# A mixed attention and gated-MLP kernel: x loaded in whole rows, key weights by feature rows, gates of two segments at a time, and a new order

## The chip, the cores and the metric

The kernel runs on one core of a Trainium2 chip. A core has five engines with an instruction stream each: TensorE (PE, matrix products into PSUM), VectorE (DVE), ScalarE (ACT), GpSimd (POOL) and SyncE (SP, which here only issues transfers). Transfers run on 16 DMA engines; SP and ACT each feed a queue of them. Engines wait for each other by semaphores. The metric is the device time of one execution in microseconds.

## The reference

x is 2048 tokens of 512 features, in four segments of 512 tokens. One branch is attention with 32 heads of 16 features, causal inside a segment, plus a linear-attention memory that carries over from segment to segment; the other is a gated MLP. A sigmoid of x times gate_w mixes them for each token.

```python
g = sigmoid((x * gate_w).sum(-1, keepdims=True))
# a: for each segment s, with phi(t) = where(t > 0, t + 1, exp(t))
a_dot = softmax(q_s @ k_s.T * 0.25 + causal) @ v_s
a_mem = (phi(q_s) @ M) / (phi(q_s) @ z + 1e-6)
o_s   = sigmoid(beta) * a_mem + (1 - sigmoid(beta)) * a_dot
M, z  = M + phi(k_s).T @ v_s, z + phi(k_s).sum(tokens)
a = o @ wo
b = (gelu(x @ w_gate) * (x @ w_up)) @ w_down        # 512 -> 1792 -> 512
return g * a + (1 - g) * b
```

## The kernel before

Everything is a list of named tasks, and the engines' streams are cut from one order of all tasks that stands in the file as text (`ORDER`, from line 852). A word such as `Q0_1a:2` places the task Q0_1a and gives its PSUM bank; `Kev0_0:a` says that ACT does this eviction, `:d` that DVE does. `Sched.schedule` (line 120) reads it, and `Emitter` (line 143) derives from the tiles that each instruction reads and writes which semaphore it waits for. Nothing is decided at run time: an engine takes its instructions in the order of the text.

Names of tasks carry the segment first. K, Q, V are projections (`project`, line 467): a product of 4 matmuls, 512 columns wide, in two tasks a and b, into one of four PSUM banks (`psD`), and an eviction (Kev, Qev, Vev). kpada and kpadb spread the keys under masks into kD. `st` (line 595) are score products, four at a time on 32 rows of the array, into the one large PSUM buffer `psX`; `exp` (line 601) turns 2048 columns of it on ACT into `pt`, `msk` (line 607) masks on POOL, and `pv` (line 638) multiplies with the values. The next `st` may only write psX when the `exp` before has read it. G and U are the two MLP products, `gd` and `gelu` the gelu on ACT, `h` (line 687) their product on DVE, `out` (line 700) the product with w_down, `wo` (line 716) the product with wo; `wev` scales the MLP part by 1 - g, `oev` (line 720) adds g times the attention part, and `dma` (line 723) stores 128 tokens. `mz`, `nz` and `nd` are the memory's products; `phk`, `phq` the feature map phi in three steps a, b, c; `ktr` its transpose by DMA; `vsh` (line 501) a copy of the values shifted by 64 partitions.

At the start x of segment 0 is loaded into a free `pt` buffer in four pieces of 256 tokens by 256 features, two on SP and two on ACT, and wk in four pieces of 256 feature rows by 256 columns, interleaved with them; wq follows in four pieces on SP. `turn_x0` (line 766) transposes x on TensorE (`xtr0`), two pieces at a time, and DVE and ACT evict it to xT (`xev0`). The key product of segment 0 (line 475) runs in eight tasks: 128 key features by 256 tokens each. Until the weights are there, TensorE runs matmuls on constants (`wake0`, `wake1`, line 366). x of the segments 1 to 3 comes by four transposing transfers each (`ld_xt`, line 328).

What stands behind each other on SP: four pieces of x and wk, four of wq, wv (waits for the last piece of x), beta, gate_w, the halves of wg (the first waits for wq, the second for wv), the four transposed pieces of x of segment 1, four vsh, then wu and the rest.

`gates` (line 412) computes g for one segment: 16 matmuls with one column of gate_w as the stationary operand into four partitions of a bank, a 32 by 32 block transpose and a minimum on DVE (`gz`), exp on ACT (`gr`), and three small steps on DVE (`go`) to g and 1 - g. gate_w itself is loaded as four rows, transposed by TensorE (`gwtr`, line 742) and copied by DVE (`gwev`).

At the end, output tile 15 alone is made and stored in two halves, one from SP and one from ACT.

Of the kernel before, what the change touches and what calls it, by code (L numbers as in the profile page):

```python
# [10 lines left out]
F32 = mybir.dt.float32  # L11
# [224 lines left out]
def _build(es, nc, A_x, A_wq, A_wk, A_wv, A_wo, A_beta, B_w_gate, B_w_up, B_w_down, gate_w, out):  # L236
# [39 lines left out]
    gt = sb("gt", [P, P], F32)  # L276
# [31 lines left out]
    def bk(s):  # L308
        return ("bank", s)
# [12 lines left out]
    gw4, ball = omem[0:4, 0, 0:P], omem[:, 1, 0:H]  # L322
    stage = (R_PT - 1,)

# [3 lines left out]
    def ld_xt(s, behind="wo30"):  # L328
        for kb in range(4):
            load(f"x{s}_{kb}", SP, lambda e, kb=kb: e.dma_start_transpose(  # L330
                xT[s % R_XT][:, kb, :], A_x[0, s * 512:(s + 1) * 512, kb * 128:(kb + 1) * 128]),
                [("xT", s % R_XT, kb, h) for h in range(2)], issue=1.31, size=0.28, wait=[("ld", behind)])
# [6 lines left out]
    for nm, w, a in (("wk", wk, A_wk), ("wq", wq, A_wq)):  # L339
        for h in range(2):  # L340
            c = slice(256 * h, 256 * h + 256)
            for k, eng in enumerate((SP, ACT if nm == "wk" else SP)):
                ld_w(f"{nm}{h}{k}", eng, w[:, halves[k], c], wsrc(a)[:, halves[k], c], [(nm, h, k)], 0.125)
    ld_w("gw", SP, gw4, gate_w.rearrange("(kb p) -> kb p", p=P), [("gw4",)], 0.01, ["x0_10"])
    ld_w("wv", SP, wv[:], wsrc(A_wv), [("wv",)], 0.5, ["x0_11"])
    ld_w("beta", SP, ball, A_beta.partition_broadcast(P), [("ball",)], 0.02, ["wk00"])
    ld_xt(1, "wv")
    ld_w("wg0", SP, wg[:, halves[0], :], wgr[:, halves[0], :], [("wg", 0)], 0.9, ["wq11"])
# [63 lines left out]
    def gates(s):  # L412
        sl = Slot()
        c = slice(4 * s, 4 * s + 4)

        mm = []
        for kb in range(4):
            for i in range(4):
                mm.append(I(lambda e, i=i, kb=kb: e.matmul(  # L419
                    BK[sl.i][32 * i:32 * i + 1, 0:128], gatew[:, kb:kb + 1],  # L420
                    xT[s % R_XT][:, kb, :].rearrange("p (q j r) -> p j q r", j=4, r=32)[:, i],
                    start=(kb == 0), stop=(kb == 3), tile_position=(0, 32 * i)),
                    [*x_of(s % R_XT, kb), ("gatew",)], [bk(sl)]))
        one(f"gate{s}", PE, 0.26, mm)
        one(f"gz{s}", DVE, 0.36, [
            I(lambda e: e.transpose(gt[:, :], BK[sl.i][:, 0:128]), [bk(sl)], [("gt",)]),
            I(lambda e: e.tensor_scalar(gz[:, c], gt[:, 0:128:32], ZMAX, None, ALU.min), [("gt",)], [("gz", s)])])
        one(f"gr{s}", ACT, 0.2, [I(lambda e: e.activation(gr[:, c], gz[:, c], ACTF.Exp), [("gz", s)], [("gr", s)])])
        one(f"go{s}", DVE, 1.2, [
            I(lambda e: e.tensor_scalar(gr1[:, c], gr[:, c], 1.0, None, ALU.add), [("gr", s)], [("gr1", s)]),  # L430
            I(lambda e: e.reciprocal(omgt[:, c], gr1[:, c]), [("gr1", s)], [("omgt", s)]),
            I(lambda e: e.tensor_tensor(gtok[:, c], gr[:, c], omgt[:, c], ALU.mult), [("gr", s), ("omgt", s)],
              [("gtok", s)]),
        ])

    def x_of(i, kb):
        return [("xT", i, kb, h) for h in range(2)]
# [29 lines left out]
    def project(s):  # L467
        b, b3 = s % 2, s % R_XT
        for t in range(4):
            if s == 0:  # L470

                sl = Slot()
                for h in range(2):
                    c = slice(256 * h, 256 * h + 256)
                    one(f"K0_{t}{'ab'[h]}", PE, 2 * T_MM, [I(lambda e, i=i, t=t, c=c, sl=sl: e.matmul(  # L475
                        BK[sl.i][:, c], wk[:, i, t * 128:(t + 1) * 128], xT[0][:, i, c], start=(i == 0), stop=(i == 3)),
                        [("xT", 0, i, h), ("wk", t // 2, i // 2)], [bk(sl)]) for i in range(4)])
            else:
                sl = dense(f"K{s}_{t}", lambda i, t=t: wk[:, i, t * 128:(t + 1) * 128], lambda i: xT[b3][:, i, :],
                           lambda i, t=t: [*x_of(b3, i), ("wk", t // 2, i // 2)], 4)  # L480
# [3 lines left out]
            for nm, ap, mk in (("kpada", kD[b][:, t, :, 0:64], maskA), ("kpadb", kD[b][:, t, :, 64:128], maskB)):  # L484
# [4 lines left out]
                       lambda i, t=t: [*x_of(b3, i), ("wq", t // 2, i // 2)], 4)  # L489
# [14 lines left out]
        gates(s)  # L504
# [50 lines left out]
    def memory_write(s):  # L555
# [3 lines left out]
        for t in range(4):  # L559
# [4 lines left out]
        sl = Slot()  # L564
        one(f"mz{s}", PE, 0.45, [I(lambda e, c=c, kt=kt, g=g, sl=sl: e.matmul(  # L565
# [10 lines left out]
                [("mzacc",), ("gphm",)], [("mzq",)])])  # L576
        one(f"zq{s}", POOL, 0.25, [I(lambda e: e.tensor_tensor(
# [112 lines left out]
    def outputs(s):  # L690
        for qt in range(4):
# [4 lines left out]
            for pi, (a, z) in enumerate(((0, 3), (3, 6), (6, 8), (8, 11), (11, 14))):  # L696
                mm = []
                for fb in range(a, z):
# [8 lines left out]
                    [bk(sl), ("omgt", s)], [("wds", wi)])]),  # L707
                (DVE, 0.66, [I(lambda e, sl=sl, gt=gt, wi=wi: e.tensor_scalar(
                    wds[wi][:, :], BK[sl.i][:, :], omgt[:, gt:gt + 1], None, ALU.mult),
                    [bk(sl), ("omgt", s)], [("wds", wi)])])], L_DVE)  # L710
            last = gt == 4 * NSEG - 1
            parts = (slice(0, 256), slice(256, 512)) if last else (slice(0, 512),)
            ko = [[("ost", oi, 0)], [("ost", oi, 1)]] if last else [[("ost", oi, 0), ("ost", oi, 1)]]
            for ci, c in enumerate(parts):
# [7 lines left out]
                        op0=ALU.mult, op1=ALU.add), [bk(so), ("gtok", s), ("wds", wi)], ko[ci])])  # L722
                one(f"dma{gt}_{ci}", (SP, ACT)[ci], 0.5, [I(lambda e, gt=gt, oi=oi, c=c: e.dma_start(
                    out[0, gt * 128:(gt + 1) * 128, c], ost[oi][:, c]), ko[ci], [("out", gt, ci)],
                    dma_sem=sem(f"s_out{gt}_{ci}"))], lat=2.0)
                outs.append(f"s_out{gt}_{ci}")
# [3 lines left out]
    def head_gates():  # L730
# [10 lines left out]
        sg = Slot()  # L741
        one("gwtr", PE, T_TR, [I(lambda e: e.transpose(BKbf[sg.i][:, 0:4], gw4, ident[0:4, 0:4]),
                                 [("gw4",), ("omem", 0), ("ident",)], [bk(sg)])])
        one("gwev", DVE, 0.1, [I(lambda e: e.tensor_copy(gatew[:, :], BKbf[sg.i][:, 0:4]), [bk(sg)], [("gatew",)])])
# [21 lines left out]
    def turn_x0():  # L766
        xs = pt[stage[0]]
        xbf = XALL.bitcast(BF)
        for h in range(2):
            for k in range(2):  # L770
                sl = Slot() if h == 0 else None
                key, held = (bk(sl), []) if h == 0 else (("Xq", k), [("X", s0)])
                dst_of = (lambda sl=sl: BKbf[sl.i][:, 0:512]) if h == 0 else (
                    lambda k=k: xbf[:, 1024 * k + 1024:1024 * k + 1536])
                one(f"xtr0_{2 * h + k}", PE, 4 * T_TR, [I(lambda e, q=q, kb=kb, dst_of=dst_of: e.transpose(
                    dst_of()[:, 256 * (kb % 2) + 128 * (q % 2):256 * (kb % 2) + 128 * (q % 2) + 128],
                    xs[:, q, kb * 128:(kb + 1) * 128], ident[:, :]), [("xs", 0, h, k), ("pt", stage[0]), ("ident",)],
                    [key]) for kb in (2 * k, 2 * k + 1) for q in (2 * h, 2 * h + 1)])
                dst = xT[0][:, halves[k], 256 * h:256 * h + 256]
                src = lambda dst_of=dst_of: dst_of().rearrange("p (k c) -> p k c", k=2)  # L780
                wr = [("xT", 0, kb, h) for kb in (2 * k, 2 * k + 1)]
                task(f"xev0_{2 * h + k}", [
                    (ACT, 0.477, [I(lambda e, dst=dst, src=src: e.activation(dst, src(), ACTF.Copy), [key, *held], wr)]),
                    (DVE, 0.335, [I(lambda e, dst=dst, src=src: e.tensor_copy(dst, src()), [key, *held], wr)])], L_DVE)
# [3 lines left out]
    for s in range(NSEG):  # L788
        if s == NSEG - 1:
            ld_xt(s)  # L790
# [62 lines left out]
ld_x0_00 ld_x0_01 ld_wk00 ld_wk01 ld_x0_10 ld_x0_11 ld_wk10 ld_wk11 ident causal1 causal0 consts masks wake0:0 ld_wq00  # L853
ld_wq01 ld_wq10 ld_wq11 ld_wv ld_beta ld_gw ld_wg0 ld_wg1 ld_x1_2 ld_x1_1 ld_x1_0 ld_x1_3 causal vones0 xtr0_0:0
xtr0_1:3 xev0_0:d xev0_1:a wake1 K0_1a:1 K0_0a:2 xtr0_2 xtr0_3 xev0_2:d xev0_3:a K0_2a:3 K0_3a:0 K0_0b K0_1b K0_2b
K0_3b Kev0_0:a Kev0_2:d Kev0_1:a kpadb0_1 phka0_0 Q0_1a:2 Q0_0a:1 Q0_0b Kev0_3:a phkb0_0 kpada0_0 kpada0_1 phka0_2
# [104 lines left out]
```

## Time and profile before

| | |
|---|---|
| runs, us | 266.31, 265.62, 266.41; median 266.31 |
| profiled execution | 266.57 us, span of its instructions 264.8 us, TensorE clock 1.00 |
| TensorE busy | 255.4 us of the span, 2792 matmuls |
| VectorE, ScalarE, GpSimd busy | 204.7, 207.2, 95.6 us |
| dearest group off TensorE | exp, 72 x 1.876 us = 135.1 us |
| DMA | 14.92 MB, HBM reads 8.14 MB, most of it in the first 60 us |

The span runs from the first to the last instruction; the time of a run is a little longer. TensorE's matmuls are pipelined: a 512-column matmul shows as 380 ns, but the next one starts 216 ns later, so a busy share says little by itself, and the start times and waits have to be read. A line such as `x8` merges eight instructions. The number in brackets behind it is how long the engine was idle before, and who released it.

### The profile page before, as it was taken

To read this page: it belongs to the slowest core of one execution; us is meant where nothing else is said; L and a number is where in the kernel's file an instruction comes from. 1 tells how busy PE (TensorE), PEld (TensorE's weight loads), DVE (VectorE), ACT (ScalarE), POOL (GpSimd) and SP (SyncE) were. 2 spreads that over 40 slices of the span, in tenths; PEclk is the share of its full clock that TensorE was granted. 3 is DMA by queue.
4 is the path that set the end of the run, shared out by engine and by line. 5 is a ranking of instruction groups with operands and counts; after the bars stand their busy time and mean duration, and the time that the engine had idled before them with its cause. 6 is when DMAs were issued, how large, how long until landed. Compare 5 with 4: busy or idle time off the path is not lost.

```text
span 264.8 us, 6603 instructions
## 1 busy us (share of the span) xinstructions
PE 255.4 (96%) x2792; PEld 112.4 (42%) x2830; DVE 204.7 (77%) x389; ACT 207.2 (78%) x170; POOL 95.6 (36%) x159
## 2 busy tenths in 40 slices
PE   7999999999999999999999999999999999999995
PEld 4634434444444443444434344444344443444442
DVE  1557576678967669999797998897987797958975
ACT  2689879988899988979988978658889967376601
POOL 6005514046422734052254438422635035062600
DMA  6895238950045020000103000013011000010002
GB/s 196 261 219 136 80 69 146 248 154 2 0 68 108 4 62 20 2 2 1 22 0 89 15 2 2 20 42 41 2 34 33 2 2 0 2 59 2 20 2 79
DMA packets 25251, 14.92 MB, mean 56 GB/s; under 512 B 14086, under 2 KB 24198, under 8 KB 25222
## 3 DMA queue, kind: packets, MB, share of 16 engines
q1 hardware_dynamic: 23990, 13.91, 23.3%
q10 hardware_dynamic: 1232, 0.59, 0.8%
q8 instruction: 22, 0.36, 0.6%
q14 instruction: 7, 0.06, 0.1%
HBM read 8.14 MB, written 2.10 MB: 39 GB/s over the span
## 4 chain that ended last, share of the span: by engine, by line
PE 88%; DVE 5%; issue 2%; DMA 2%; ACT 1%; SPq 1%; DVEq 0%; ACTq 0%
PE psD L450 49%; PE psD L700 18%; PE psX L595 8%; PE psD L638 5%; PE psD L716 5%; DMA wk<-in_A_wk_dram 2%; DVE gb L687 1%; PE psD L475 1%; DVE kT L443 1%; PE psD L565 1%; ACT pt L601 1%; SPq L326 1%; DVE oT L657 1%; DVE tT L518 0%; PE psD L419 0%
## 5 line engine op out<-in xcount | busy, mean ns | idle before, releaser
L601 ACT ACTIVATE pt<-psX 128x2048 bf16<-128x2048 f32 x72 | 135.1, 1876 | 32.3 <-PE psX L595 31.7
L607 POOL TENSOR_TENSOR pt<-pt,ctri 128x256 bf16<-128x256 bf16 x128 | 90.5, 714 | 152.8 <-ACT pt L601 148.4
L450 PE MATMUL psD<-xT,wu 128*128 128x512 bf16 x212 | 55.5, 380 | 1.6 <-issue 1.3
L450 PE MATMUL psD<-xT,wg 128*128 128x512 bf16 x217 | 54.8, 380 | 1.0 <-issue 0.5
L700 PE MATMUL psD<-wd,gb 128*128 128x512 bf16 x214 | 52.5, 379 | 1.4 <-issue 1.0
L687 DVE TENSOR_TENSOR gb<-psD,gb 128x512 bf16<-128x512 f32 x56 | 37.4, 682 | 12.0 <-PE psD L450 11.6
L518 DVE STREAM_TRANSPOSE tT<-psD 128x512 f32<-128x512 f32 x35 | 23.4, 694 | 11.4 <-PE psD L638 11.2
L700 PEld LDWEIGHTS psD<-wd,gb 128*128 128x128 bf16 x224 | 20.7, 98 | 25.8 <-issue 2.8
L450 PEld LDWEIGHTS psD<-xT,wg 128*128 128x128 bf16 x224 | 20.3, 98 | 26.1 <-issue 2.8
L450 PEld LDWEIGHTS psD<-xT,wu 128*128 128x128 bf16 x224 | 20.1, 98 | 25.5 <-issue 3.7
L595 PE MATMUL psX<-qT,kD 32*128 32x192 bf16 (+7 forms) x512 | 28.6, 287 | 0.2
L595 PEld LDWEIGHTS psX<-qT,kD 32*128 32x128 bf16 x512 | 8.2, 92 | 25.9 <-ACT pt L601 19.5
L649 DVE SCALAR_TENSOR_TENSOR ob<-tT,gq,rc 128x256 bf16<-128x256 f32 x32 | 18.2, 567 | 1.1
L638 PE MATMUL psD<-pt,vnat 64*17 64x128 bf16 (+7 forms) x512 | 18.7, 283 | 0.0
L443 DVE CAST gb<-psD 128x512 bf16<-128x512 f32 x23 | 15.7, 683 | 3.7 <-PE psD L450 3.6
L638 PE MATMUL psD<-pt,vsh 64*17 64x128 bf16 (+7 forms) x512 | 18.3, 283 | 0.0
L450 PE MATMUL psD<-wv,xT 128*128 128x512 bf16 x61 | 17.3, 381 | 0.3 <-issue 0.3
L450 PE MATMUL psD<-xT,wq 128*128 128x512 bf16 x62 | 16.7, 380 | 0.1
L716 PE MATMUL psD<-wo,oT 128*128 128x512 bf16 (+1 forms) x66 | 15.7, 366 | 0.3 <-issue 0.2
L638 PEld LDWEIGHTS psD<-pt,vnat 64*17 64x17 bf16 x512 | 11.6, 86 | 8.7 <-issue 3.8
L678 ACT ACTIVATE gb<-psD 128x512 bf16<-128x512 f32 x28 | 14.7, 602 | 0.3 <-PE psD L450 0.3
L720 DVE SCALAR_TENSOR_TENSOR ost<-psD,gtok,wds 128x512 bf16<-128x512 f32 (+1 forms) x17 | 11.9, 712 | 2.5 <-PE psD L716 2.2
(99 smaller groups left out, 251.2 us busy)
## 6 DMA issues: line engine op xcount, KB each, us to landing
out_dram<-ost SPq DMA_DIRECT2D x15, 128.0 KB, 1.7
wg<-in_B_w_gate_dram SPq DMA_DIRECT2D x2, 896.0 KB, 6.5
wu<-in_B_w_up_dram SPq DMA_DIRECT2D x2, 896.0 KB, 5.5
wd<-in_B_w_down_dram SPq DMA_DIRECT2D x2, 896.0 KB, 7.5
vsh<-vnat SPq DMA_DIRECT2D x16, 68.0 KB, 2.1
wq<-in_A_wq_dram SPq DMA_DIRECT2D x4, 128.0 KB, 4.7
wv<-in_A_wv_dram SPq DMA_DIRECT2D x1, 512.0 KB, 3.8
pt<-in_A_x_dram SPq DMA_DIRECT2D x2, 128.0 KB, 3.5
```

What stands on the lines that cost most here:

```text
L443: (DVE, 0.60, [I(lambda e: e.tensor_copy(dst, src()), [bk(sl), *reads], writes)]),
L450: one(f"{name}{'abcd'[h // 2]}", PE, 2 * T_MM, [I(lambda e, i=i: e.matmul(BK[sl.i][:, :], lhs(i), rhs(i), start=(i == 0), stop=(i == n - 1 ...
L518: one(f"tp{name}", DVE, 0.605, [I(lambda e, ts=ts, bank=bank: e.transpose(tT[ts.i][:, :], bank()), [key], [("tT", ts)])])
L595: ins.append(I(lambda e, c=c, kb=kb, ncol=ncol, c0=c0, g=g: e.matmul(XALL[:, g * 512 + c0:g * 512 + c0 + ncol], kD[b][quad(g), c, kb, :], ...
L601: one(f"exp{s}_{name}", ACT, 2048 * 0.000833 + 0.05, [I(lambda e: e.activation(pt[slot][:, :, :], xin, ACTF.Exp, scale=ATT_SCALE), [("X", ...
L607: ins.append(I(lambda e, mv=mv: e.tensor_tensor(mv, mv, cm, ALU.mult), [("pt", slot), ("causal",)], [("pt", slot)]))
L638: ins.append(I(lambda e, kb=kb, slot=slot, c0=c0, n=n, g=g, c=c, r0=r0, sl=banks[j], va=va: e.matmul(BK[sl.i][32 * c:32 * c + 17, 64 * kb: ...
L649: I(lambda e, ts=ts, t=t, j=j, dst=dst: e.scalar_tensor_tensor(out=dst, in0=t_rows(ts, 16), scalar=gq[:, 2 * t + j:2 * t + j + 1], in1=rc_ ...
L678: one(f"gd{s}_{ft}", ACT, 0.485, [I(lambda e, gi=gi, f=f, sl=sl: e.activation(gb[gi][:, f, :], BK[sl.i][:, :], ACTF.Gelu_apprx_tanh), [bk( ...
L687: one(f"h{s}_{ft}", DVE, 0.605, [I(lambda e, sl=sl, gi=gi, f=f: e.tensor_tensor(gb[gi][:, f, :], BK[sl.i][:, :], gb[gi][:, f, :], ALU.mult ...
L700: mm.append(I(lambda e, fb=fb, gi=gi, f=f, q=q, sl=sl: e.matmul(BK[sl.i][:, :], gb[gi][:, f, q], wd[:, fb, :], start=(fb == 0), stop=(fb = ...
L716: one(f"wo{s}_{qt}_{ci}", PE, 4 * T_MM / len(parts), [I(lambda e, kb=kb, q=q, so=so, c=c: e.matmul(BK[so.i][:, c], oT[:, kb, q], wo[:, kb, ...
```

## The change

x of segment 0 is loaded in four pieces of 128 tokens with whole rows (1 KB each), in turn from SP and ACT; wk in four pieces of 128 feature rows with all 512 columns (1 KB rows), after x, and wq in two. On each of the two queues both pieces of x stand ahead of both pieces of wk. wv waits for the third piece of x instead of the last, and the first half of wg for the first half of wq.

```diff
+    for q in range(4):
+        ld_w(f"x0_{q}", (SP, ACT)[q % 2], pt[stage[0]][:, q, :], A_x[0, 128 * q:128 * q + 128, :], [("xs", q)], 0.125)
+    for i in range(4):
+        ld_w(f"wk{i}", (SP, ACT)[i % 2], wk[:, i, :], wsrc(A_wk)[:, i, :], [("wk", i)], 0.125)
     for h in range(2):
-        for k, eng in enumerate((SP, ACT)):
-            c = slice(256 * k, 256 * k + 256)
-            ld_w(f"x0_{h}{k}", eng, pt[stage[0]][:, halves[h], c],
-                 A_x[0, 256 * h:256 * h + 256, c].rearrange("(q p) d -> p q d", p=P), [("xs", 0, h, k)], 0.125)
...
-    ld_w("gw", SP, gw4, gate_w.rearrange("(kb p) -> kb p", p=P), [("gw4",)], 0.01, ["x0_10"])
-    ld_w("wv", SP, wv[:], wsrc(A_wv), [("wv",)], 0.5, ["x0_11"])
+        ld_w(f"wq{h}", SP, wq[:, halves[h], :], wsrc(A_wq)[:, halves[h], :], [("wq", h)], 0.25)
+    load("gw", SP, lambda e: e.dma_start(gatew[:, :], gate_w.rearrange("(kb p) -> p kb", p=P),
+                                         allow_slow_non_contiguous=True), [("gatew",)], wait=[("ld", "x0_2")])
+    ld_w("wv", SP, wv[:], wsrc(A_wv), [("wv",)], 0.5, ["x0_2"])
```

x is transposed piece by piece, four transposes and one eviction each; in the new order DVE does all four evictions, the first piece goes through a bank and the others through psX. The key product of the first 256 tokens runs feature row block by feature row block over all four banks at once; the other 256 tokens follow key block by key block. The constant matmuls are nine ahead of the first transpose and none later.

```diff
+        if s == 0:
+            k0 = [Slot() for _ in range(4)]
+            for i in range(4):
+                one(f"K0_k{i}", PE, 2 * T_MM, [I(lambda e, i=i, t=t: e.matmul(
+                    BK[k0[t].i][:, 0:256], wk[:, i, t * 128:(t + 1) * 128], xT[0][:, i, 0:256], start=(i == 0),
+                    stop=(i == 3)), [("xT", 0, i, 0), ("xT", 0, i, 1), ("wk", i)], [bk(k0[t])]) for t in range(4)])
...
-    for i, cols in enumerate(([512] * 5 + [128] * 2, [128] * 6)):
+    for i, cols in enumerate(([512] * 5 + [128] * 3, [128] * 1)):
```

The gates of the segments 0 and 1, and of 2 and 3, are computed together: 32 matmuls into the upper half of the bank in which the memory product `mz` of segment 0 or 1 is then made, and one visit of each DVE and ACT step. gate_w comes by one transfer of 512 single elements, straight into the layout that the matmuls need; its transpose and copy are gone.

```diff
-    def gates(s):
-        sl = Slot()
-        c = slice(4 * s, 4 * s + 4)
...
+    def gate_products(h, sl):
+        one(f"gate{h}", PE, 0.5, [I(lambda e, i=i, kb=kb, s=s: e.matmul(
+            BK[sl.i][32 * i:32 * i + 1, 256 + 128 * (s % 2):384 + 128 * (s % 2)], gatew[:, kb:kb + 1],
+            xT[s % R_XT][:, kb, :].rearrange("p (q j r) -> p j q r", j=4, r=32)[:, i],
+            start=(kb == 0), stop=(kb == 3), tile_position=(0, 32 * i)),
+            [*x_of(s % R_XT, kb), ("ld", "gw")], [bk(sl)])
+            for s in (2 * h, 2 * h + 1) for kb in range(4) for i in range(4)])
...
+        if s < 2:
+            gate_products(s, sl)
```

(Here the `s` of the call is 0 or 1 and stands for the pair.) At the end, output tile 14 is made in two halves as well, and stored whole; tile 15 is made and stored in halves as before.

```diff
+            split = gt >= 4 * NSEG - 2
             last = gt == 4 * NSEG - 1
-            parts = (slice(0, 256), slice(256, 512)) if last else (slice(0, 512),)
+            parts = (slice(0, 256), slice(256, 512)) if split else (slice(0, 512),)
```

`ORDER` is another text throughout: banks, engines of the evictions and the place of nearly every task differ. Its start, and the part around the first read of x of segment 1 (`Q1_3a`):

```diff
+ld_x0_0 ld_x0_1 wake0:0 ident wake1 xtr0_0:2 ld_x0_2 ld_x0_3 xtr0_1 xtr0_2 xev0_0:d xev0_1:d ld_wk0 xtr0_3 ld_wk2
+xev0_3:d ld_wk1 K0_k0:2013 xev0_2:d K0_k1 ld_wk3 K0_k2 K0_k3 ld_wq0 K0_3b ld_wq1 K0_2b ld_wv Kev0_3:d Kev0_2:a phka0_2
+K0_0b masks Kev0_0:d K0_1b Kev0_1:a ld_beta phkb0_2 Q0_3a:3 kpadb0_1 Q0_0a:1 ld_wg0 Q0_0b consts causal1 Qev0_0:a
...
+Vev0_0:d V0_3b V0_2a:0 st0_0B:0 phkc0_2 V0_2b Vev0_2:d ld_x1_1 Vev0_3:a G0_2a:1 G0_1a:3 exp0_0B G0_1b Gev0_1:a G0_3a:2
+ld_x1_0 st0_0C:0 Q1_3a:0 G0_0a:3 G0_2b Gev0_2:d G0_3b ld_x1_3 exp0_0C Q1_3b msk0_0B phka0_0 vsh0_01 vsh0_21 Gev0_3:d
```

On SP the new gate_w transfer stands behind three of the four vsh of segment 0, and ahead of the fourth and of the second half of wu; the rest of SP's row has the same order up to the first transfer of x of segment 3. The count of ScalarE's table loads is the same in both orders.

More of the change, by code (lines that the diff above doesn't have):

```diff
@@ L321, in _build, with x_of @@
     halves = (slice(0, 2), slice(2, 4))
-    gw4, ball = omem[0:4, 0, 0:P], omem[:, 1, 0:H]
+    ball = omem[:, 1, 0:H]
     stage = (R_PT - 1,)
+    def x_of(i, kb):
+        return [("xT", i, kb, q) for q in range(4)]
     def ld_w(name, eng, dst, src, writes, size, wait=()):
@@ L409, in _build @@
     one("consts", POOL, 4.2, cn)
-    def gates(s):
-        sl = Slot()
-        c = slice(4 * s, 4 * s + 4)
[L416 to L433, printed above, removed]
-        ])
@@ L721, in outputs @@
                         out=ost[oi][:, c], in0=BK[so.i][:, c], scalar=gtok[:, gt:gt + 1], in1=wds[wi][:, c],
[L722 to L726, printed above, removed]
+                        op0=ALU.mult, op1=ALU.add), [bk(so), ("gtok", s // 2), ("wds", wi)], ko[ci])])
+                if last or ci == len(parts) - 1:
+                    kd, d = (ko[ci], c) if last else ([k for kk in ko for k in kk], slice(0, 512))
+                    one(f"dma{gt}_{ci}", (SP, ACT)[last and ci], 0.5, [I(lambda e, gt=gt, oi=oi, d=d: e.dma_start(
+                        out[0, gt * 128:(gt + 1) * 128, d], ost[oi][:, d]), kd, [("out", gt, ci)],
+                        dma_sem=sem(f"s_out{gt}_{ci}"))], lat=2.0)
+                    outs.append(f"s_out{gt}_{ci}")
     outs = []
@@ L768, in turn_x0 @@
         xbf = XALL.bitcast(BF)
[L769 to L784, printed above, removed]
+        for q in range(4):
+            sl = Slot() if q == 0 else None
+            key, held = (bk(sl), []) if q == 0 else (("Xq", q), [("X", s0)])
+            dst_of = (lambda sl=sl: BKbf[sl.i][:, 0:512]) if q == 0 else (lambda q=q: xbf[:, 1024 * q:1024 * q + 512])
+            one(f"xtr0_{q}", PE, 4 * T_TR, [I(lambda e, q=q, kb=kb, dst_of=dst_of: e.transpose(
+                dst_of()[:, 128 * kb:128 * kb + 128], xs[:, q, kb * 128:(kb + 1) * 128], ident[:, :]),
+                [("xs", q), ("pt", stage[0]), ("ident",)], [key]) for kb in range(4)])
+            dst = xT[0][:, :, 128 * q:128 * q + 128]
+            src = lambda dst_of=dst_of: dst_of().rearrange("p (k c) -> p k c", k=4)
+            wr = [("xT", 0, kb, q) for kb in range(4)]
+            task(f"xev0_{q}", [
+                (ACT, 0.477, [I(lambda e, dst=dst, src=src: e.activation(dst, src(), ACTF.Copy), [key, *held], wr)]),
+                (DVE, 0.335, [I(lambda e, dst=dst, src=src: e.tensor_copy(dst, src()), [key, *held], wr)])], L_DVE)
     turn_x0()
@@ L788, in _build @@
     for s in range(NSEG):
[L789 to L790 removed]
+        if s == 1:
+            ld_xt(3)
         project(s)
```

206 lines of the change are left out of this document (100 added, 106 removed).

## The prediction

> **What bounds the kernel now.** I read the page's busy shares first, then TensorE's own waits from 9.9 us to the end, then its timeline at the start, the transfers of the first 20 us and VectorE's timeline at the end.
>
> ```profile
> span 264.8 us, 6603 instructions
> ...
> PE 255.4 (96%) x2792; PEld 112.4 (42%) x2830; DVE 204.7 (77%) x389; ACT 207.2 (78%) x170; POOL 95.6 (36%) x159
> ```
>
> ```profile
> PE psD L450 <- issue: 2.1, 13, 0.2
> PE psD L700 <- issue: 1.0, 6, 0.2
> PE psD L450 <- DVE gb L687: 0.5, 3, 0.2
> PE psD L450 <- DVE oT L657: 0.2, 1, 0.2
> ```
>
> The second fence is the list of TensorE's waits between 9.9 and 262 us: name, total, times, longest. No idle time is over 0.2 us, about the 0.216 us pitch of one 512-column matmul, so most of these are single records that the trace lost. From the first query projection on, TensorE runs without a stall. Time can come from three places only: the start, TensorE's own work, and what follows its last matmul; and every new wait in between is paid in full.
>
> ```profile
> 3.61 0.83 PE L775 MATMUL psD<-ident,pt 128*128 128x128 bf16 x8 [0.25 <-DMA pt<-in_A_x_dram]
> ...
> 4.74 1.22 PE L475 MATMUL psD<-xT,wk 128*128 128x256 bf16 x8
> 6.21 0.79 PE L775 MATMUL psX<-ident,pt 128*128 128x128 bf16 x8 [0.24 <-DMA pt<-in_A_x_dram]
> 7.11 3.01 PE L475 MATMUL psD<-xT,wk 128*128 128x256 bf16 x24
> 10.17 3.40 PE L450 MATMUL psD<-xT,wq 128*128 128x512 bf16 x15
> ```
>
> TensorE's timeline (start, length): eight key matmuls run at 4.74, then it waits for the second half of x (6.21) and for wk (7.11). From 7.54 to 10.12 the chain of waits has 22 of them, so the pitch is 0.11; the last 24 end at 9.95. Of 16 query matmuls 15 are recorded; 16 x 0.216 back from the value matmul at 13.41 also gives **9.95** as the start of Q0.
>
> **The start (gain 1.0; ends 0.2 and 1.3).**
>
> ```profile
> wk<-in_A_wk_dram ACTq DMA_DIRECT2D x1, 128.0 KB, 5.1
> ...
> q1 hardware_dynamic: 548, 0.26, 111.0%
> ...
> q1 hardware_dynamic: 139, 0.14, 80.7%
> ```
>
> The first line is the last quarter of wk, issued at 2.39: landed at 2.39 + 5.1 = 7.5. The other two are the SP queue in windows 6.0 to 6.9 (512-byte packets) and 8.5 to 9.0 (1 KB): packets, MB, share of 16 engines. A packet took 0.9 x 16 x 1.11 / 548 = 29 ns, against 0.5 x 16 x 0.807 / 139 = 46 ns; a kilobyte so costs 58 ns before and 46 now, a factor of 0.79. First bytes flowed at about 2.2, so x and wk took 5.3 us; times 0.79 is 4.2, landing at 6.4. Part of it is the landing, which does not shrink: I take **6.7**. Ends: 7.5 (no gain) and 5.2 (1,024 packets x 46 ns / 16 = 2.9 us, engines never idle).
> The Trainium skill, "DMA: Bandwidth & Descriptors", section Specifications, puts the smallest transfer for line rate at 512 B, which would make the new rows no quicker; the two rows above disagree with it, and by the rule the sum would be 0.8 smaller.
>
> The rest of the new start: the first piece of x (issued at 0.81, 2.8 us to landing) is there at 3.6, as before. VectorE evicted the first transposes 0.65 us after they began (4.26); now it does all four evictions at 0.42 each, from 4.3: 4.7, 5.1, 5.5, 5.9. The first key group needs two pieces and the first 128 feature rows: 5.15. Four groups of 4 x 0.11 would end at 6.9; the fourth waits for 6.7, so it runs 6.75 to 7.2. The 16 matmuls of the second token half take 1.74: Q0 at **8.95** instead of 9.95. With all weights early it is 5.15 + 32 x 0.109 = 8.65, with wk at 7.5 it is 9.7. The longer first wake (nine matmuls, not seven) ends at about 3.4, before x; the filler it replaces ran in idle time. ScalarE loses its two x evictions, and its table load (1.28 us at 2.91) stays under the DMAs. The score group at the end of V0 needs eight key paddings and the evictions of K and Q: VectorE has 8 x 0.28 + 3 x 0.65 + 0.4 + 0.35 = 4.9 us for the 5.4 us between its first key eviction and TensorE's arrival, so this is tight but covered; without cover it costs 0.3.
>
> **TensorE's work after that (0.7 less; ends 0.3 and 0.9).** Each gate of 16 matmuls costs 0.33 in the chain of waits, 1.3 for four. Two of 32 remain, directly ahead of the memory product, which uses tiles of the same shape: 0.33 + 0.18 less a drain of about 0.1 each, 0.9 in all: 0.4 less. The small transpose of gate_w goes: its neighbours start 0.42 apart instead of 0.216, 0.2 less. Counted over both orders, changes of tile shape fall from 177 to 173; three belong to the gates, one more at 0.1 (a score group starts 0.31 after a dense matmul, 19.78 to 20.09).
> VectorE loses two gate visits (0.3 + 0.19 + 0.27 + 0.18 + 0.16 each) and a copy; it is 77% busy, so nothing comes of that. The gate weights now arrive as 512 elements of 2 bytes, issued on SP behind three of the four transfers of shifted values, about 20 us; behind them wait the fourth and wu. The fourth is first read at about 28, and its like took 2.1 us to land, so even 5 us more is hidden; gate0 itself runs at about 53. The Trainium skill ("DMA: Bandwidth & Descriptors", Rules for kernel authors) says that such a pattern costs one descriptor per element; no run here shows one yet, and nothing above depends on it.
>
> **The end (0.2 less; ends 0 and 0.3).**
>
> ```profile
> 260.36 0.75 DVE L708 TENSOR_SCALAR wds<-psD,omgt 128x512 f32<-128x512 f32 x1 [0.98 <-PE psD L700]
> 261.22 1.53 DVE L720 SCALAR_TENSOR_TENSOR ost<-psD,gtok,wds 128x512 bf16<-128x512 f32 x3
> ```
>
> TensorE's last matmul ends at 262.05, the last output eviction at 262.75: three evictions stand back to back from 261.22, the last one 0.2 behind its matmul. Split in halves, and with the scaling of the last tile on ScalarE (0.69, free there), they keep up: 0.2. Tile 14 still leaves in one transfer, ahead of tile 15's halves.
>
> **New waits (0.6 more; ends 0 and 2.2).** First, the four transposed loads of x for segment 1.
>
> ```profile
> xT<-in_A_x_dram SPq DMA_TRANSPOSE x1, 7.2
> ...
> q8 instruction: 1, 0.02, 3.5%
> ```
>
> The first line is the list of issues in window 14 to 15: the third of them, issued at 13.73, landed 7.2 later, at 20.95, and the old order reads it at 21.94. The new order has 40 dense matmuls and three score groups (9.85 us) ahead of that read, where the old had 12.0: it comes at 8.95 + 9.85 = **18.8**. The loads move up too: wv no longer waits for the second half of x (issued 6.56, landed 10.4) but for its third piece, so it goes out at about 4.2 and lands behind wq, at 2.2 + 2,048 x 46 ns / 16 + 0.6 = 8.7; the second half of wg waits for it, the four loads stand behind that on SP. They land 1.7 earlier, near 19.3. Against that, the last two arrived two microseconds after the others, beside a load of code (the q8 line, window 18 to 20), which they may miss this time (about 18.2). I take 0.3 of stall.
> Second, the score buffer: 0.45 from scores to exp, 1.88 exp, 0.06 to the next score: 2.38 is the shortest pitch seen. In the new order the pair around the first memory product (st0_2C, st0_2D) has about 2.2 us of TensorE work, and behind the second gelu batch ScalarE is 3.4 us late with 5.2 us to make it up (two exps and one 1.05 us exp): 0.1 to 0.7. The old order had the like at the last gelu batch and lost nothing. I take 0.3.
>
> **Sum.** -1.0 - 0.7 - 0.2 + 0.6 = -1.3. The profiled execution took 266.57 (span 264.8 and 1.8 around it): 265.3; the median of the runs is 266.31, 0.26 lower: **265.0**.
>
> **Rivals.**
> *The loads of segment 1 come no earlier* (slower). If SP's four transposes again take 7 us to issue behind wg, and land at 21.0, Q1 waits 21.0 - 18.8 = 2.2 in place of my 0.3: 266.31 - 1.9 + 2.2 + 0.3 = 266.9, and 267.2 with the score buffer at 0.6, which the wait does not help. It is slower from a landing after 20.4 on, by over 0.3% from 21 on. For it: the old margin was only 1.0 and the read moves up 3.1. Against: wv and wg are issued about 2 us earlier.
> *Long rows bring nothing* (no change). wk at 7.5, Q0 at 9.7: -0.2 - 0.7 - 0.2 + 0.6 = -0.5, 265.8. For it: 5.1 us to landing is mostly not packets (16 engines need 3.7 for 2,048 of 29 ns). Against: 29 and 46 ns.
> *The order stalls where it is tight* (no change): the second wait at its end of 0.7 and 0.6 for banks held by late gelus, 1.3 in place of 0.3: 266.31 - 1.9 + 0.3 + 1.3 = 266.0. For it: three gelu batches meet later exps than before. Against: the old order had the same pitch and no stall.
>
> **How the numbers follow.** The measurement tells 0.3%, 0.8 us, from no change. Forecast 0.56, loads of segment 1 late 0.20, long rows 0.16, order 0.08: faster 0.56, same 0.24, slower 0.20. Lowest: -1.3 - 0.9 - 0.3 = -2.5, 263.8; at the top the slower rival, 267.2. The forecast's own range is 263.8 to 265.5.
>
> **What would show it.** Q0 at 8.95 and wk landed by 6.7 (right), or the fourth key group waiting for wk past 7.2 (second rival). TensorE's idle time ahead of the first matmul with x of segment 1 (18.8): 0.3, or 2. In the list of TensorE's waits any entry over 0.25 after 9 us is a new stall. The last output eviction should start with TensorE's end. I am wrong if Q0 moves up by a microsecond and the end does not.

## The result, and the profile after

The changed kernel takes 268.69 us (median of four runs, 268.53 to 269.26) against 266.31 (265.62 to 266.41): 2.4 us slower, ratio 1.0099 with a 95% interval from 1.0076 to 1.0121. The profiled execution took 268.53 us, its span is 266.8.

From the page of the changed kernel: the span, the busy times, and the chain that ended last, by engine; below it the same chain in the kernel before.

```profile
span 266.8 us, 6600 instructions
...
PE 254.8 (96%) x2790; PEld 112.4 (42%) x2829; DVE 208.0 (78%) x381; ACT 206.4 (77%) x166; POOL 99.8 (37%) x159
...
PE 78%; DVE 16%; issue 3%; DMA 1%; SPq 0%
```

```profile
PE 88%; DVE 5%; issue 2%; DMA 2%; ACT 1%; SPq 1%; DVEq 0%; ACTq 0%
```

TensorE has 0.6 us less to do and the span is 2.0 us longer. VectorE's part of the chain rises from 5% to 16%. And it is busy 3.3 us longer although it has eight instructions fewer: single instructions have become longer.

The list of TensorE's waits from 8 to 265 us (releaser, total, times, longest):

```profile
PE psD L444 <- issue: 2.4, 15, 0.2
PE psD L444 <- DVE kT L437: 1.3, 1, 1.3
PE psD L700 <- issue: 1.3, 8, 0.2
PE psD L444 <- DVE kD L483: 0.7, 1, 0.7
```

Where no entry was over 0.2 before, two are now, both behind VectorE. TensorE's timeline at the start, then at the longer of the two:

```profile
5.56 1.91 PE L466 MATMUL psD<-xT,wk 128*128 128x256 bf16 x16 [0.76 <-DMA wk<-in_A_wk_dram]
7.30 1.91 PE L472 MATMUL psD<-xT,wk 128*128 128x256 bf16 x16
9.27 3.40 PE L444 MATMUL psD<-xT,wq 128*128 128x512 bf16 x15
...
37.59 0.38 PE L444 MATMUL psD<-xT,wg 128*128 128x512 bf16 x1 [0.16 <-issue]
39.24 1.04 PE L444 MATMUL psD<-xT,wg 128*128 128x512 bf16 x4 [1.27 <-DVE kT L437]
```

The first recorded query matmul starts at 9.27 instead of 10.17, so 0.9 us is gained by then; the rest of the run gives back 2.9. The two waits are 2.0 of it. VectorE's timeline ahead of 39.24 shows the first place:

```profile
35.15 2.25 DVE L740 COPY betab<-omem 32x8 bf16<-32x8 bf16 x7
37.43 0.69 DVE L437 CAST qT<-psD 128x512 bf16<-128x512 f32 x1
38.16 0.43 DVE L454 TENSOR_SCALAR phq<-qT 128x1024 bf16<-128x1024 bf16 x1
38.50 0.68 DVE L437 CAST kT<-psD 128x512 bf16<-128x512 f32 x1
```

Seven small copies take 2.25 us, and the eviction of kT whose bank TensorE waits for stands behind them. In the kernel before they took 0.95:

```profile
20.37 0.95 DVE L737 COPY betab<-omem 32x8 bf16<-32x8 bf16 x7
```

Singly they take about 160 ns; three of the seven took 533 to 641 in the changed kernel, where a mask multiply runs on GpSimd at the same time. The old order started its masks at 22.5 and in batches, the new one multiplies each block right behind its exp, from 15.9 on. That became the first theory. The second place, 86.08, looks alike. Three VectorE instructions ahead of it, while four masks run on GpSimd from 82.17 on:

```profile
82.12 0.99 DVE L649 SCALAR_TENSOR_TENSOR ob<-tT,gq,rc 128x256 bf16<-128x256 f32 x1
83.04 0.88 DVE L454 TENSOR_SCALAR phk<-kT 128x1024 bf16<-128x1024 bf16 x1
83.85 0.75 DVE L483 TENSOR_SCALAR kD<-kT,maskA 128x512 bf16<-128x512 bf16 x1
```

The same three take 0.48, 0.42 and 0.35 us in e3 below, which has no masks.

### The profile page after: what moved, and what is told of

Read it like the earlier page. It is cut to its first block, busy times and chain, and to the rows that moved or that the text cites. A ratio compares the mean times of both kernels' runs of the same rounds, so it can differ in the third digit from the quotient of the medians.

```text
span 266.8 us, 6600 instructions
## 1 busy us (share of the span) xinstructions
PE 254.8 (96%) x2790; PEld 112.4 (42%) x2829; DVE 208.0 (78%) x381; ACT 206.4 (77%) x166; POOL 99.8 (37%) x159
## 4 chain that ended last, share of the span: by engine, by line
PE 78%; DVE 16%; issue 3%; DMA 1%; SPq 0%
PE psD L444 43%; PE psD L700 15%; PE psX L595 7%; PE psD L638 6%; PE psD L717 5%; DVE gb L687 3%; DVE tT L514 2%; DVE ob L649 2%; DMA wk<-in_A_wk_dram 1%; DVE oT L657 1%; DVE phq L457 1%; DVE gb L437 1%; DVE ob L655 1%; DVE betab L740 1%; PE psD L466 1%
## 5 line engine op out<-in xcount | busy, mean ns | idle before, releaser
L607 POOL TENSOR_TENSOR pt<-pt,ctri 128x256 bf16<-128x256 bf16 x128 | 94.5, 743 | 144.5 <-ACT pt L601 139.9
L444 PE MATMUL psD<-xT,wu 128*128 128x512 bf16 x219 | 56.4, 380 | 0.7 <-DVE gb L687 0.2
L444 PE MATMUL psD<-xT,wg 128*128 128x512 bf16 x212 | 52.4, 379 | 3.5 <-issue 1.3
L700 PE MATMUL psD<-wd,gb 128*128 128x512 bf16 x214 | 53.3, 380 | 1.5 <-issue 1.3
L649 DVE SCALAR_TENSOR_TENSOR ob<-tT,gq,rc 128x256 bf16<-128x256 f32 x32 | 19.9, 621 | 1.1
L638 PE MATMUL psD<-pt,vnat 64*17 64x448 bf16 (+7 forms) x512 | 18.9, 283 | 0.0
L638 PE MATMUL psD<-pt,vsh 64*17 64x320 bf16 (+7 forms) x512 | 18.2, 283 | 0.0
L437 DVE CAST gb<-psD 128x512 bf16<-128x512 f32 x21 | 14.0, 676 | 5.2 <-PE psD L444 5.2
L444 PE MATMUL psD<-wv,xT 128*128 128x512 bf16 x61 | 16.7, 380 | 0.4 <-issue 0.3
```

Of the source, the lines that this page charges most:

```text
L437: (DVE, 0.60, [I(lambda e: e.tensor_copy(dst, src()), [bk(sl), *reads], writes)]),
L444: one(f"{name}{'abcd'[h // 2]}", PE, 2 * T_MM, [I(lambda e, i=i: e.matmul(BK[sl.i][:, :], lhs(i), rhs(i), start=(i == 0), stop=(i == n - 1 ...
L607: ins.append(I(lambda e, mv=mv: e.tensor_tensor(mv, mv, cm, ALU.mult), [("pt", slot), ("causal",)], [("pt", slot)]))
L638: ins.append(I(lambda e, kb=kb, slot=slot, c0=c0, n=n, g=g, c=c, r0=r0, sl=banks[j], va=va: e.matmul(BK[sl.i][32 * c:32 * c + 17, 64 * kb: ...
L649: I(lambda e, ts=ts, t=t, j=j, dst=dst: e.scalar_tensor_tensor(out=dst, in0=t_rows(ts, 16), scalar=gq[:, 2 * t + j:2 * t + j + 1], in1=rc_ ...
L700: mm.append(I(lambda e, fb=fb, gi=gi, f=f, q=q, sl=sl: e.matmul(BK[sl.i][:, :], gb[gi][:, f, q], wd[:, fb, :], start=(fb == 0), stop=(fb = ...
```

## The experiments

Medians: four executions for e15, five for e16, six for e5 and e9, nine to twelve for the other experiments. The kernel before was measured again beside each group of experiments and moved a little (266.38 to 266.54); the difference to that median stands beside each time.

| run | us | to before | ratio, 95% interval |
|---|---|---|---|
| the change itself | 268.69 | +2.4 | 1.0099 (1.0076 to 1.0121) |
| e1 changed, masks late | 267.38 | +0.9 | 1.0040 (1.0021 to 1.0060) |
| e2 before, masks early | 266.54 | +0.1 | 1.0002 (0.9991 to 1.0014) |
| e3 changed, no masks | 265.89 | -0.6 | 0.9978 (0.9967 to 0.9989) |
| e4 before, no masks | 266.60 | +0.1 | 1.0009 (0.9999 to 1.0019) |
| e5 changed, betab early | 267.76 | +1.4 | 1.0065 (1.0042 to 1.0088) |
| e6 changed, betab early and masks late | 267.01 | +0.6 | 1.0038 (1.0018 to 1.0059) |
| e7 new head alone | 266.23 | -0.2 | 1.0005 (0.9987 to 1.0022) |
| e8 all new parts, old order | 265.88 | -0.5 | 0.9991 (0.9975 to 1.0007) |
| e9 changed, masks to scratch | 269.14 | +2.6 | 1.0113 (1.0090 to 1.0136) |
| e10 as e8, longer wake | 266.01 | -0.5 | 0.9981 (0.9973 to 0.9990) |
| e11 as e6, longer wake | 266.67 | +0.1 | 1.0006 (0.9998 to 1.0015) |
| e12 new gates and tail, old head and order | 266.28 | -0.3 | 0.9991 (0.9981 to 1.0000) |
| e13 before, no masks, paddings twice | 266.61 | +0.1 | 1.0010 (1.0000 to 1.0019) |
| e14 changed, no masks, paddings twice | 267.60 | +1.1 | 1.0054 (1.0031 to 1.0077) |
| e15 before, no masks, betab three times | 267.60 | +1.1 | 1.0045 (1.0030 to 1.0060) |
| e16 changed, no masks, betab three times | 268.10 | +1.6 | 1.0088 (1.0048 to 1.0127) |

### Masks moved and masks left out (e1 to e4)

In e1 and e2 only the `msk` words of `ORDER` move; e3 and e4 drop them and the multiply:

```diff
-            ins.append(I(lambda e, mv=mv: e.tensor_tensor(mv, mv, cm, ALU.mult), [("pt", slot), ("causal",)],
-                         [("pt", slot)]))
-        one(f"msk{s}_{name}", POOL, 0.70 * len(steps), ins)
```

e1:

> The changed kernel with one thing put back: the mask multiplies keep their place on GpSimd's list as in the kernel before (in batches, a late one first, ahead of the attention product that needs them), where the changed kernel masks each score block behind its exponential; every other step keeps its new place. Theory C (contention: a mask on GpSimd stretches VectorE's SBUF-only instructions, and the new order lets masks run while VectorE is what TensorE waits for): the stall of 1.3 us behind the seven betab copies goes, the copies take about 0.95 us in all instead of 2.25, and 1.3 to 2.4 us of the loss come back: 266.3 to 267.4 us. Theory O (the new order gives VectorE its work too late whatever GpSimd does): 268.3 to 269 us, the same as the changed kernel. A third outcome, over 269.5 us, would say that late masks hold up the attention products in this order.

e2:

> The kernel before with one thing changed: each mask multiply stands right behind its exponential on GpSimd's list instead of in batches. Theory C: VectorE's SBUF-only instructions are stretched from the first exponential on (at about 16 us rather than 22), the seven betab copies at 20 us no longer take 160 ns each but 500 to 640, and the kernel gets 0.5 to 2 us slower: 266.8 to 268.3 us. Theory O: no change, 266.0 to 266.6 us.

e3:

> The changed kernel without the mask multiplies: the multiplication of the causal masks into the exponentials is left out, so that GpSimd does nothing beside most of VectorE's work. Its time is to be read against the kernel before with the same left out (the next run). Theory C: this kernel is 0.8 to 1.8 us faster than that one, as the head and TensorE's stream alone would have it. Theory O: it is still about 2 us slower than that one.

e4:

> The kernel before without the mask multiplies (the multiplication of the causal masks into the exponentials is left out), as the yardstick for the run above. Theory C: 0 to 1 us faster than the kernel before (265.3 to 266.3 us), since VectorE is on 5% of its chain; the changed kernel without masks is faster than this one. Theory O: about the same, and the changed kernel without masks is about 2 us slower than this one.

Late masks bring back 1.5 us of the 2.4, and without masks the changed kernel is 0.7 us faster than the kernel before without them, a little less than the 0.8 expected at least. So the masks on GpSimd decide. But e2 and e4 missed: the old order loses nothing by early masks, though its betab copies did get longer, and gains nothing without any. The betab line of VectorE's timeline in e1, then in e2:

```profile
35.55 0.94 DVE L740 COPY betab<-omem 32x8 bf16<-32x8 bf16 x7
```

```profile
19.68 1.50 DVE L737 COPY betab<-omem 32x8 bf16<-32x8 bf16 x7
```

How much longer VectorE's work becomes is read from two busy rows with the same 381 instructions, here that of e3:

```profile
PE 254.1 (96%) x2790; PEld 113.3 (43%) x2829; DVE 194.9 (74%) x381; ACT 206.2 (78%) x166; POOL 5.4 (2%) x31
```

208.0 - 194.9: masks cost VectorE 13.1 us in the new order; the same difference for the old order is 204.7 - 195.5 = 9.2. Which instructions: the groups on tile kD in the changed kernel (shortest/median/longest in ns, first and last start), then in e3.

```profile
L483 DVE TENSOR_SCALAR kD<-kT,maskB x16: 307/348/778, 9.9 to 189.5; 128x512 bf16<-128x512 bf16 x16
L483 DVE TENSOR_SCALAR kD<-kT,maskA x16: 304/348/753, 10.2 to 186.6; 128x512 bf16<-128x512 bf16 x16
```

```profile
L483 DVE TENSOR_SCALAR kD<-kT,maskB x16: 310/346/405, 10.5 to 187.0; 128x512 bf16<-128x512 bf16 x16
L483 DVE TENSOR_SCALAR kD<-kT,maskA x16: 311/346/486, 10.8 to 183.7; 128x512 bf16<-128x512 bf16 x16
```

The same for the mix of memory and attention on tile ob, changed kernel and e3, and for the evictions from PSUM on tile qT in the changed kernel:

```profile
L649 DVE SCALAR_TENSOR_TENSOR ob<-tT,gq,rc x32: 483/486/990, 41.6 to 257.5; 128x256 bf16<-128x256 f32 x32
```

```profile
L646 DVE SCALAR_TENSOR_TENSOR ob<-tT,gq,rc x32: 483/485/486, 40.3 to 254.6; 128x256 bf16<-128x256 f32 x32
```

```profile
L437 DVE CAST qT<-psD x8: 652/691/737, 11.7 to 138.1; 128x512 bf16<-128x512 f32 x8
```

The longest of the instructions that read SBUF are twice as long, while the medians hardly move (348 against 346 ns): some are stretched, most are not. Evictions from PSUM stay where they are. The Trainium skill, "SBUF — State Buffer", section SBUF: two separate sides, says that VectorE in a two-port mode or with two SBUF inputs and GpSimd take a shared pair of ports by turns, each for a whole instruction; these rows agree, and the added 400 ns of a kD or betab instruction is more than half of a mask's mean of 714 (before) to 743 ns (changed).

### Is it the stretching, or the wait for the masks? (e9)

In e9 the multiplies stay on GpSimd and write to a scratch tile, so the attention uses exponentials without masks. The lines that make the tile are left out here:

```diff
-            ins.append(I(lambda e, mv=mv: e.tensor_tensor(mv, mv, cm, ALU.mult), [("pt", slot), ("causal",)],
-                         [("pt", slot)]))
+            ins.append(I(lambda e, mv=mv, k=ring[f"msk{s}_{name}"][len(ins)]: e.tensor_tensor(
+                mscr[:, 4 * k:4 * k + 4, :], mv, cm, ALU.mult), [("pt", slot), ("causal",)],
+                [("mscr", ring[f"msk{s}_{name}"][len(ins)])]))
```

> The changed kernel with every mask multiply kept on GpSimd, in its place, of its size, but writing its product to a scratch tile: the masks are left out of the attention result, so no attention product waits for GpSimd. This parts two readings of the run without masks (2.8 us faster than the changed kernel). Theory C (GpSimd's instructions stretch VectorE's, and TensorE then waits for VectorE): nothing changes, 268.2 to 269.2 us. Rival W (what costs is the wait of the attention products for their masks, which this kernel does not have either): 265.6 to 266.3 us, as without masks.

It is as slow as the changed kernel (+2.6 against +2.4), with its waits (TensorE's list in e9):

```profile
PE psD L447 <- DVE kT L440: 1.0, 1, 1.0
PE psD L447 <- DVE kD L486: 0.7, 1, 0.7
PE psD L447 <- DVE gb L696: 0.7, 3, 0.4
PE psD L447 <- DMA xT<-in_A_x_dram: 0.4, 1, 0.4
```

No attention product waits for GpSimd here, and the loss stays: it goes through VectorE. The last line is the wait that the first rival of the forecast named; it was absent in the profiled execution of the changed kernel, and stands in two more of the nine profiles of the new order, with 0.2 in e14 and 0.6 in e16.

### Why the old order does not mind (e13 to e16)

```diff
-                      [("kT", 0, t), (mk.name,)], [("kD", b, t, nm)])])
+                      [("kT", 0, t), (mk.name,)], [("kD", b, t, nm)]) for _ in range(1 + (s > 0))])
...
-        for c in range(4):
+        for c in (*range(4), *range(4), *range(4)):
```

The first edit is that of e13 and e14, the second that of e15 and e16.

e13:

> The kernel before without the mask multiplies (left out, as above: 266.6 us), and every key padding of segments 1 to 3 done twice: 24 VectorE instructions of about 0.27 us more, 6.5 us in all, with nothing on GpSimd to stretch them. Theory S (the old order leaves VectorE room): 266.3 to 267.0 us. Theory P (the orders have the same room): the same added time as in the next run.

e14:

> The changed kernel without the mask multiplies (left out: 265.9 us) and the same 24 paddings done twice, 6.5 us of VectorE's work more. Theory S (the new order leaves VectorE no room): 1.0 to 2.5 us more, 266.9 to 268.4 us. Theory P: as little or as much more as in the run before it.

e15:

> The kernel before without mask multiplies (left out), the seven betab copies done three times at their place at 20 us: 14 copies more, 1.9 us of VectorE's work at one place. Theory S: 266.3 to 267.0 us. Theory P: about 1.3 us more, as where masks stretched them in the changed kernel.

e16:

> The changed kernel without mask multiplies (left out), the betab copies done three times at their place at 35 us: 1.9 us more of VectorE's work where TensorE waited 1.3 us in the changed kernel. Theory S: most of it shows, 267.0 to 267.9 us. Theory P: the same added time as in the run before it.

With no masks on GpSimd, 24 more paddings (VectorE's busy time rises by 7.5 us in the old order, 8.1 in the new) cost the old order nothing, 266.60 to 266.61, and the new one 1.7, 265.89 to 267.60. That is theory S: the new order leaves VectorE no room. TensorE's longest wait in e14 is at 185.62:

```profile
PE psD L444 <- DVE tT L514: 1.1, 1, 1.1
```

The copies at one place add 1.97 us of work (2.92 for 21 against 0.95): the old order shows 1.0 of it, the new one 2.2. Both expectations missed, e16 by 0.2. At 20 us the old order has about 1 us of room, not 2. The 2.2 holds more than the copies, since two of e16's five executions took over 270 and its profiled one has the 0.6 named above; the wait behind the copies is 1.9 there, all of what was added. TensorE's waits behind VectorE in e15, then in e16:

```profile
PE psD L450 <- DVE gb L443: 1.0, 1, 1.0
```

```profile
PE psD L444 <- DVE kT L437: 1.9, 1, 1.9
```

### Putting the two edits into the changed kernel (e5, e6)

In e5 and e6 the word `betab` moves behind `Vev0_2:d`; e6 has the masks of e1 as well.

e5:

> The changed kernel with one task moved: the seven betab copies stand on VectorE's list behind the eviction of V0_2, where VectorE idles from 17.7 to 20.5 us, instead of at 35.2 us, where TensorE waited 1.3 us behind them. Masks keep the changed kernel's places. If the stall there is the price of these stretched copies, 1.0 to 1.4 us come back: 267.3 to 267.7 us, and TensorE's longest wait on VectorE falls from 1.3 to 0.5 us or less. If VectorE has too much to do in that stretch anyway, the wait stays with the next instruction and the time stays over 268.2 us.

e6:

> Both edits in the changed kernel: the masks in the places of the kernel before (as in the run with late masks, 267.4 us) and the betab copies early. If each edit removes the same stall (the copies were stretched by masks), little is added: 267.0 to 267.5 us. If they remove different ones, 266.0 to 266.6 us.

Moving the copies alone brings 1.0 us, close to the stall of 1.3; the second wait, of 0.7, stays as it was, where at most 0.5 was expected. On top of late masks it brings 0.3: mostly the same stall.

The medians of e1 and e6 are of twelve executions of which three and four are long ones (see the late clock below). TensorE's time from the start of its first recorded query matmul to the end of its last matmul leaves the start out, where executions differ:

| profiled execution of | us |
|---|---|
| before, e2, e4, e7, e13 | 251.9 |
| e8, e10, e12 | 251.7 |
| the change | 254.9 |
| e5 | 253.7 |
| e1 | 252.9 |
| e6, e11 | 252.3 |
| e3 | 251.4 |

So the new order without masks is the shortest of all, and the two edits together leave 0.9 of the 3.5 us that masks cost it. In e11 no wait of TensorE in this stretch is over 0.2. Set beside e3's, its start times fall back by 0.2 us at 147.8, 0.2 at 161.2 and 0.4 at 192.4, each time with a VectorE instruction as the releaser. The change has five such steps of 0.2 to 0.4, 1.4 in all, between 149 and 195 us, beside 1.3 and 0.6 at its two waits. Why the new order has less room at these places was not followed further.

### The parts without the new order (e7, e8, e12)

e7 is the kernel before with the new loads, `turn_x0` and `K0_k`; e8 has all new functions and the old order behind the head; e12 is e8 with the old head.

e7:

> The kernel before with the head of the change alone: x in four pieces of whole rows, key weights by feature rows, the keys over four banks; everything from the first key eviction on stands in the old order, with the gate transposition and the old tail. If the head's gain reaches the end (1.0 us at the first query in the forecast, 0.9 in the trace), 265.2 to 265.6 us. If the rest of the old order gives it back at its waits, 266.0 to 266.6 us.

e8:

> All parts of the change (head, gates of two segments per visit beside the memory products, gate weights loaded transposed, the last row tile but one in two halves) with the tasks in the order of the kernel before. If the parts are worth what the forecast gave them (-1.0, -0.7 and -0.2) and the loss lies in the new order alone, 264.4 to 265.2 us, the fastest of all. If the parts themselves cost (a gate visit that holds a bank, the slower gather of the gate weights), 265.8 to 267 us.

e12:

> The kernel before with everything of the change except the new head and the new order: gates of two segments per visit, gate weights loaded transposed, the halved tile near the end. The forecast gave these parts -0.9 us (0.7 of TensorE's work, 0.2 at the end): 265.3 to 265.6 us. The run of all parts in the old order against that of the head alone gives 0.3: then 265.9 to 266.2 us.

The head alone brings 0.2, gates and tail 0.3, all together 0.5 (the intervals of e7 and e8 hold no change, that of e10 does not). e7 and e8 came out in the less hopeful of their two ranges, though not for the reasons given there: behind the start TensorE needs the same 251.9 us in e7 as before, and less in e8. e12 is 0.1 above its range. So the parts cost nothing, but they are worth under half of the 1.9 that the forecast gave them.

Why the head is worth so little shows in the start of the first recorded query matmul, read from TensorE's timeline of every profiled execution. Old head (before, e2, e4, e12, e13, e15): 10.17, 9.48, 9.67, 10.44, 10.12, 9.84, median 9.98. New head (the change, e1, e3, e5, e6, e7, e8, e9, e10, e11, e14, e16): 9.27, 9.66, 9.84, 9.50, 10.80, 11.64, 9.84, 9.81, 9.66, 9.88, 9.78, 9.38, median 9.80. The changed kernel's profile caught the best of twelve. In the new head nothing can start before the first piece of wk, which landed between 5.4 and 6.1; then 32 matmuls of 0.109 take 3.5, and the first of the 16 query matmuls, 0.2, is missing from every trace.

### A late clock (e7, e8, e10, e11)

Two of e7's twelve executions took 268.0, the others 265.9 to 266.4, and the profile is one of the two. TensorE's timeline in e7, then in e8 (265.87):

```profile
6.25 3.57 PE L469 MATMUL psD<-xT,wk 128*128 128x256 bf16 x16 [0.91 <-DVE ctri L387]
9.62 1.97 PE L475 MATMUL psD<-xT,wk 128*128 128x256 bf16 x16
```

```profile
6.13 1.91 PE L466 MATMUL psD<-xT,wk 128*128 128x256 bf16 x16 [0.76 <-DMA wk<-in_A_wk_dram]
7.87 1.91 PE L472 MATMUL psD<-xT,wk 128*128 128x256 bf16 x16
```

All weights were there by 7 us in e7, yet its first 16 key matmuls start 0.213 apart instead of 0.109: half the clock, 1.7 us. The first record of a granted clock in its trace is at 9.73 (at 3.68 for the change, 5.90 for e8). Ahead of them TensorE idled for 0.9 us; it did so in e3 too, which kept its clock, so the gap does not always have this effect. e10 and e11 fill it:

```diff
+    one("wake2", PE, 1.0, [I(lambda e: e.matmul(
+        XALL[:, 0:128], nc.const_aps.tensor(1.0, [P, P], BF), nc.const_aps.tensor(1.0, [P, 128], BF),
+        start=True, stop=True), [], [("Xw",)]) for _ in range(9)])
```

e10:

> All parts of the change in the old order, and nine 128-column wake matmuls more behind the transpositions of x, where TensorE idled from about 5.1 us until the first piece of the key weights landed at about 6.1. In the profiled execution of the run with the new head alone (268.0 us) the granted clock came only at 9.73 us and the first 16 key matmuls took 0.213 us each instead of 0.109, 1.7 us lost; in the others it came by 6. Theory L (the idle gap ahead of the keys lets the clock come late, in some executions): the executions of 267.5 us and more are gone, all between 265.4 and 266.4, median 265.7 to 265.9. If the gap has nothing to do with it, one to three of twelve are still 1.7 us longer.

e11:

> The changed kernel with late masks and early betab copies (four of whose twelve executions took 268.1 to 268.4 us, the rest 266.0 to 267.5), and the nine wake matmuls behind the transpositions of x. Theory L: no execution over 267.5, median 266.3 to 266.8. If the late clock is not due to the gap, a third stays at 268.

```profile
5.11 0.69 PE L369 MATMUL psX<-const-bfloat16-1.0 128*128 128x128 bf16 x9
5.96 1.91 PE L469 MATMUL psD<-xT,wk 128*128 128x256 bf16 x16 [0.16 <-DMA wk<-in_A_wk_dram]
```

This is e10: the nine matmuls lie in the gap. None of its 11 executions is over 266.5, none of e11's 11 over 267.1. Of the kernels with the new head and no filler (the change, e1, e3, e5 to e9, e14, e16), 17 of 90 executions were 1.4 to 2.4 us above the median of the others of their kernel, of the 49 with the old head (e2, e4, e12, e13, e15) none. If the filler did nothing, 22 in a row without one would have a chance of 0.81 to the power of 22, 1%. A clock late by 16 matmuls was seen in one trace only, and one of e6's (267.46) had a late piece of wk instead, so not every long execution need have it. The median does not gain in e10 (266.01 and 265.88). The Trainium skill, "TensorE: Matmul & The Clock Gate", section What's actually happening, says that the full clock needs about 3.4 us of sustained work in a window that runs by itself, so that its start differs between executions, by 500 ns either way. It does differ here, by more: from 3.68 to 9.73 in the traces. The window itself shows in no run.

## Why the prediction was wrong, point by point

- **The failed step** is the term for new waits, +0.6. It holds two, for the loads of segment 1 and for the score buffer, and none behind VectorE. VectorE's work was added up for one stretch, with instructions of undisturbed length (8 x 0.28 for the paddings); of the rest the working says "it is 77% busy, so nothing comes of that" (of instructions that VectorE loses), and the new places of GpSimd's masks have no price at all. The loss is there: 268.69 against 265.88 for the same parts in the old order, 2.8 us. It comes from masks that stretch VectorE's instructions (e3, e9) in an order that leaves VectorE no room (e13, e14). A share of 77% said nothing on either: with 203.0 us of VectorE's work in both e13 and e14, one order waits and the other does not.
- **The start** was given -1.0 and is worth about -0.2. That the change's own profile shows 0.9 was luck, the earliest of twelve; there the working's own sign of being wrong came true, a Q0 that moves up by a microsecond and an end that does not. The step that was mis-sized is the first key group at 5.15, when "two pieces and the first 128 feature rows" would be there: it started at 5.56 in the change's profile and at 5.5 to 6.3 in the others. The end of wk's loading, on which the working spent its rows, was not the limit: but for 0.1 to 0.2 us K0 ran through behind its first piece in ten of twelve executions (e6 waited 1.0 for a later one, e14 0.3).
- **TensorE's work and the end**, -0.7 and -0.2: e12 shows 0.3 (0 to 0.5) for both, of which TensorE's work is 0.2 (251.9 to 251.7). What was mis-sized is what the four old gates cost, 0.33 each and 1.3 in all: set beside those of the kernel before, e12's start times gain 0.9 where these gates stood, lose 0.44 at each of the two new ones, as forecast, and gain 0.2 at the transpose of gate_w. The end came as forecast, in the two lines below from the changed kernel: the last eviction ends at 264.68, 0.5 behind the last matmul (264.16), where it was 0.7.

```profile
262.25 1.91 PE L717 MATMUL psD<-wo,oT 128*128 128x256 bf16 x16
262.89 1.79 DVE L721 SCALAR_TENSOR_TENSOR ost<-psD,gtok,wds 128x256 bf16<-128x256 f32 x4 [1.41 <-PE psD L717]
```

- **The new waits**, +0.6: the first query of segment 1 ran at 18.98 without a wait (forecast 18.8 and 0.3; 0.2 to 0.6 in e9, e14 and e16), and ScalarE is not in the chain at all, so nothing shows that the score buffer cost anything. Both named waits were right to be small; the one that came was not on the list. The gate weights landed 3.0 us after their issue, hidden as forecast.
- **The rivals.** The one on an order that "stalls where it is tight" had the right kind of loss, with the wrong engine and 1.6 us of waits in place of 2.8. The slower rival had the sign without the cause.

## What to carry to other kernels

An engine off the critical path at three quarters of its time can still be the one that TensorE waits for: before an order is changed, add up per stretch what VectorE must finish for TensorE, and look which of its instructions read SBUF while GpSimd works. A batch of GpSimd's multiplies where VectorE has room is free, the same ones spread behind their producers need not be. A gain at the start, where transfers and the clock decide, should be measured over several executions before it is booked.

## What the runs showed that was not expected

The same masks cost VectorE 9.2 us of busy time and the kernel nothing in one order, 13.1 us and about 3 in the other. And a gap of 0.9 us ahead of the first real matmuls went with half the clock and 1.7 us in one profiled execution; with nine matmuls on constants in the gap none of 22 executions was long.
